# A fused attention and two-layer gated network on one core: most of the gate and value weights prepared later, and the last attention product spread along block 7

## The chip, the core and the metric

The kernel runs on one core of a Trainium2 chip. The core has a matrix engine (TensorE, PE in the profile, with its weight loads as PEld), a vector engine (VectorE, DVE), a scalar engine (ScalarE, ACT), a general engine (GpSimd, POOL) and a queue engine (SyncE, SP). SP and POOL issue the transfers; sixteen DMA engines move the bytes. Each engine takes its instructions in the order in which they stand in its own queue. The metric is the device time of one execution in microseconds (us), the median of three runs.

## The reference, cut to what matters

```python
# attention: 8 batches, 8 heads, 576 tokens, head 64; keys and values are means over 8 tokens
k_p, v_p = mean of 8 tokens of k, v                 # 72 of each
attn = softmax(q @ k_p.T / 8) @ v_p
x = attn as 4608 tokens x 512
# first network
h = ((x @ w1) * (x @ w2)) @ w3                      # 512 -> 1024 -> 1024
y = h @ w_out                                       # 1024 -> 512
# second network
xn = y / sqrt(mean(y*y) + 1e-6) * rms_g
out = (silu(xn @ w_gate) * (xn @ w_val)) @ w_out    # 512 -> 1536 -> 512
```

The weights arrive as 64-bit floats and the result is 32-bit. The kernel computes every large product as three passes of a split operand: high times high, high times low, low times high.

## The kernel before, in words

The 4608 tokens are worked as nine blocks of 512 tokens, numbered 0 to 8, while the attention has eight batches of 576 tokens, numbered 0 to 7. Block i holds the end of batch i-1 and the start of batch i.

**First pass.** `ab(i, m, s)` is one product of block i: twelve matmuls into one PSUM bank, for weight s (0 is w1, 1 is w2) and output part m. A block has sixteen of them. With s = 0 ScalarE copies the bank out (line 571); with s = 1 VectorE multiplies the two (line 574, to tile `hh` or `hl`) and SP stores the result. `w3` and `w_out` were multiplied into one matrix ahead of it (tiles `wph`, `wpl`).

**The attention of the next batch runs between these products.** `positions(i)` is a list of sixteen places, one behind each `ab`. Place 1 holds the last part of the product with the values for block i+1 (`av_step`) and the loads of the keys of the batch after (`C.k0`). Places 1 to 12 hold the scores, the exponentials, the division and the transposes of five token tiles (VectorE's lines 337, 351 to 353 and 368, tile `aT`). Place 13 holds the part of the new batch that lies in block i+1. `av_step` multiplies on TensorE (line 428, bank `pa`), casts on ScalarE (line 435, tile `xh`) and takes the rest on VectorE (line 436, tile `xl`); the block's own matmuls read `xh` (lines 104 and 106) and `xl` (line 105). Places 14 and 15 prepare the keys of the batch after: `C.k1` sums over tokens on VectorE (lines 253 and 257, tile `kv`), `C.kT` turns them on TensorE (line 288), `C.Q` turns the queries (line 307).

**The weights of the second network are prepared in between, too.** `gv_steps(G, s, kp)` makes a group of eight steps for one part of `w_gate` or `w_val`; there are twelve groups (G = 0, 1, 2). Each loads two raw pieces of 0.5 MB (line 127), converts them from 64 to 32 bits (ScalarE's lines 144 and 147, VectorE's 159, 168 and 171), forms four differences (line 733), splits two halves into high and low (lines 100 and 101, tile `wst`) and stores them with four transfers of 0.5 MB from POOL's queue (line 750, to `wd`). A `Ticker` hands out a list of steps evenly over a number of ticks. Before, all 97 steps of the twelve groups are spread over 116 ticks, one behind each `ab` of blocks 1 to 8; what is left is done behind the sixth product of block 8.

**Second pass.** After block 8 the products h are read back (`h_load`, line 1182, tile `hr`), split (`h_split`: ScalarE's line 100, VectorE's line 101, tile `hb`) and multiplied with `wph` and `wpl`. A pair is two parts m, 24 matmuls; the pass has 36 pairs, nine blocks of four. `h_split` is called two pairs ahead, and `hb` has four buffers. `y_end` stores a finished block. In blocks 1 to 5 of this pass a second `Ticker`, `side`, hands out the fourteen steps that convert `w_out` of the second network (twelve conversions, tile `raw`, result `of`, stores to `od`), over 40 ticks.

**Third part.** Block 0 through the second network by `gv`, blocks 1 to 8 by `quad` in pairs of blocks. It reads `wd` (`ring_load`, tile `wr`) and `od` (`o2_load`, tiles `oh`, `ol`).

What a source line calls is not yet the order on an engine: the recording layer sorts the instructions of each engine by its own estimate of when they can start. The orders shown below are those of the built programs.

Of the kernel before, what the change touches and what calls it, by code (L numbers as in the profile page):

```python
# [9 lines left out]
F32 = mybir.dt.float32  # L10
F32R = mybir.dt.float32r
# [10 lines left out]
def kernel(  # L22
# [683 lines left out]
    odram = [dram_p.tile([2, P, 4, DM], F32, name=f"od{g}") for g in range(KF2 // 4)]  # L706
    ready = set()

    def gv_steps(G, s, kp):
        w = (w_gate, w_val)[s]  # L710
        cell = {}

        def ptile(nm, dt=F32R):
            return wC_p.tile([P, 2048], dt, tag="w", name=nm)

        def quart(z):
            if "f" not in cell:
                cell["f"] = ptile("wf", F32).rearrange("p (j f c) -> p j f c", j=2, f=8)
            f = cell["f"].bitcast(I32)
            return f[:, :, 2 + 2 * z : 4 + 2 * z, :]  # L720

        def view(z):
            return z.rearrange("p (j f c) -> p j f c", j=2, f=2)

        def sums():
            f = cell["f"]
            for o, x, y in (
                ("T1", "B12", "B11"),
                ("T2", "B22", "T1"),
                ("T3", "B22", "B12"),  # L730
                ("T4", "B21", "T2"),
            ):
                nc.vector.tensor_tensor(
                    out=f[:, :, FI[o], :],
                    in0=f[:, :, FI[x], :],
                    in1=f[:, :, FI[y], :],
                    op=ALU.subtract,
                )

        def put(j):  # L740
            f = cell["f"]
            c = 2 * G + j
            st = ptile("wst").rearrange("p (f l c) -> p f l c", f=8, l=2)
            split(st[:, :, 0, :], st[:, :, 1, :], f[:, j])
            cell[j] = st

        def store(j):
            c, st = 2 * G + j, cell[j]
            for z in range(2):
                nc.gpsimd.dma_start(  # L750
                    out=wdram[s, c, z][:, :, kp],
                    in_=st[:, 4 * z : 4 * z + 4].bitcast(F32),
                )
            ready.add((s, c, kp))

        cs, raws = [], raw_halves()
        for z in range(2):
            k0 = (2 * z + kp) * P
            src = w[k0 : k0 + P, G * 512 : (G + 1) * 512]
            cs.append(Conv(src, raws, out=lambda z=z: quart(z), view=view))  # L760
            cs[z].on_act = True
        return cs, [
            cs[0].s1,
            cs[0].s2,
            cs[1].s1,
            cs[1].s2,
            sums,
            lambda: put(0),
            lambda: (put(1), store(0)),
            lambda: store(1),  # L770
        ]

    groups = [gv_steps(G, s, kp) for G in range(3) for s in range(2) for kp in range(2)]
    gv_prep = [lambda: [cs_.s0() for cs_ in groups[0][0]]]
    for n, (cs, steps) in enumerate(groups):
        if n + 1 < len(groups):
            nxt = groups[n + 1][0]
            steps[4] = lambda f=steps[4], nxt=nxt: (nxt[0].s0(), nxt[1].s0(), f())
        gv_prep += steps

    def positions(i):
        pos = [[] for _ in range(2 * KF1)]
        b = i + 1
        if b >= B:
            return pos
        A = atts[b]
        pos[1] = av_steps(i, i + 1) + [
            lambda: A.S(0, 0), lambda: A.Q(1, 0), lambda: A.S(0, 1)
        ]
        pos[2] = [lambda: A.N(0)]  # L790
        for t in range(1, NTL):
            p = 2 * t + 1
            pos[p] += [lambda t=t: A.S(t, 0)]
            if t < 4:
                pos[p] += [lambda t=t: A.Q(1 + t // 2, t % 2)]
            pos[p] += [lambda t=t: A.S(t, 1)]
            pos[p + 1] += [
                lambda t=t: A.T(t - 1, 0), lambda t=t: A.T(t - 1, 1), lambda t=t: A.N(t)
            ]
        pos[8] += [A.v]  # L800
        pos[12] += [lambda: A.T(NTL - 1, 0), lambda: A.T(NTL - 1, 1)]
        pos[13] += av_steps(b, i + 1)
        if b + 1 < B:
            C = atts[b + 1]
            pos[1] += [C.k0]
            pos[9] += [C.load_v]
            pos[10] += [lambda: C.q(0)]
            pos[14] += [C.k1, lambda: C.q(1)]
            pos[15] += [C.kT, lambda: C.Q(0, 0), lambda: C.Q(0, 1)]
        return pos  # L810

# [14 lines left out]
            st()  # L826
    xt.pop(0)

    r_p = None
    prep = Ticker(gv_prep, 2 * KF1 * (NB - 2) + 4)  # L830
    for i in range(1, NB):
        if i == NB - 2:
            for st in av_steps(i, i + 1):
                st()
            att.close()
            r_p = ctx.enter_context(tc.tile_pool(name="r", bufs=5, side="right"))
        pos = positions(i)
        for n, (m, s) in enumerate((m, s) for m in range(KF1) for s in range(2)):
            ab(i, m, s)
            for st in pos[n]:  # L840
                st()
            prep()
            if i == NB - 1 and n == 5:
                prep.flush()
                wph[:], wpl[:] = [], []
                for g in range(2):
                    for l, lst in enumerate((wph, wpl)):
                        lst.append(wtile(wC_p, "wp"))
                        nc.sync.dma_start(out=lst[g].bitcast(F32), in_=wpdram[g][l])
        xt.pop(i)  # L850
    h_put.pop(0)()

    def rtile(nm, dt=F32R):
        return r_p.tile([P, 2048], dt, tag="r", name=nm)

    o2r = {}

    def o2_jobs(g):
        cell = {}

        def row(j):
            if j == 0:
                cell["f"] = rtile("of", F32).rearrange("p (j c) -> p j c", j=4)
            return cell["f"].bitcast(I32)[:, j, :]

        def done(_):
            f = cell.pop("f")
            hl = [rtile(nm).rearrange("p (j c) -> p j c", j=4) for nm in ("of", "of")]
            split(hl[0], hl[1], f)
            for l in range(2):  # L870
                nc.gpsimd.dma_start(out=odram[g][l], in_=hl[l].bitcast(F32))

        js = [
            Conv(
                w_o2[(4 * g + j) * P : (4 * g + j + 1) * P, :],
                (r_p, "xq", 2),
                out=lambda j=j: row(j),
                then=done if j == 3 else None,
            )
            for j in range(4)  # L880
        ]
        for j in js:
            j.on_act = True
        return js
# [99 lines left out]
    def xprep(i0):  # L984
        q, rr, sc = {}, {}, {}

        def load():
            rr["r"] = raw_p.tile([P, 1024], I32, tag="raw", name="rr").bitcast(F32)
            for j in range(2):
                nc.sync.dma_start(  # L990
                    out=rr["r"][:, j * TB : (j + 1) * TB],
                    in_=rdram[i0 + j].partition_broadcast(P),
                )
            for j in range(2):
                for u in range(2):
                    if j == 0:
                        t = r_p.tile([P, 1024], I32, tag="xq", name="xq", bufs=2).bitcast(F32)
                    else:
                        t = raw_p.tile([P, 1024], I32, tag="raw", name="xq").bitcast(F32)
                    q[f"A{j + 1}{u + 1}"] = t  # L1000
                    nc.sync.dma_start(
                        out=t.rearrange("p (k t) -> p k t", k=2),
                        in_=ydram[i0 + j, 2 * u : 2 * u + 2].rearrange("k p t -> p k t"),
                    )
# [188 lines left out]
    o2 = []  # L1193
    for g in range(3):
        o2 += o2_jobs(g)
    o2 = conv_steps(o2, 1)
    for n in range(3):
        h_load(n)
    h_split(0)
    h_split(1)  # L1200
    todo = []
    side = Ticker(o2, 5 * KF1)
    xs = xn_steps(0)
    for i in range(NB):
        for m in range(KF1):
            n = i * (KF1 // 2) + m // 2
            if m % 2 == 0:
                h_load(n + 3)
                h_split(n + 2)
            t = hb[n]  # L1210
            h_t[i, m] = [t[:, l, (m % 2) * TB : (m % 2 + 1) * TB] for l in range(2)]
            c = m % 4
            second(i, m, wph[m // 4][:, c, :], wpl[m // 4][:, c, :], KF1 - 1, False)
            if m and todo:
                todo.pop(0)()
            if i == 0 and m == 4:
                ring_load(0, 1)
                ring_load(1, 1)
            if i > 0:
                side()  # L1220
            if i >= NB - 2 and m % 2 and xs:
                xs.pop(0)()
        todo = y_end(i)
# [96 lines left out]
```

## Time and profile before

| | |
|---|---|
| runs | 1677.32, 1675.08, 1678.94 us; median 1677.32 |
| profiled execution | 1674.94 us, of which the span of the trace is 1673.2 us |
| TensorE busy | 1612.5 us of the span |
| VectorE busy | 1012.9 us |
| ScalarE busy | 680.6 us |
| granted clock of TensorE, mean | 0.984 of full speed |
| moved by DMA | 322.52 MB, mean 193 GB/s |

A busy TensorE isn't a TensorE at its peak, since overlapping matmuls count as busy throughout and since its clock is granted at one of two levels. So a stage is read by three columns together: how long TensorE was idle, which clock it was granted, and how busy the engine was that it waited for. Matmuls of 512 columns are listed with 0.39 us each, but they overlap, and start 0.23 us apart.

### The profile page before, as it was taken

The numbers are of one execution on the slowest core, as the hardware profiler recorded it, in microseconds if no ns is written. First come the engines' busy times: TensorE is split into PE (matmuls) and PEld (weight loads), VectorE is DVE, ScalarE is ACT, GpSimd is POOL, SyncE is SP. The second block draws the span as 40 slices with busy tenths as digits, with TensorE's granted clock in tenths as the row PEclk, the third lists the DMA queues.
The fourth block names the chain that finished last, engine by engine and source line by source line (L and its number), as shares of the span: only waits on it lengthen the run. The fifth ranks groups of instructions, "written<-read, shape, count | busy, mean of one in ns | idle before, by whom it ended". The sixth has DMA issues, their size and how long they took to land.

```text
span 1673.2 us, 19957 instructions
## 1 busy us (share of the span) xinstructions
PE 1612.5 (96%) x7250; PEld 1285.4 (77%) x7250; DVE 1012.9 (61%) x1773; ACT 680.6 (41%) x1607; POOL 93.5 (6%) x107
## 2 busy tenths in 40 slices
PE   5899989889889999999999999999999999999999
PEld 2447768678677688888888888888888888888887
DVE  4676698898898632566526253486356735475444
ACT  4776545545445322555423243244323433234321
POOL 1001111211110100000100000000000000000000
PEclk9899999999999899999999999999999999999999
DMA  9858555756853565568556764457345836455422
GB/s 241 253 172 212 136 159 159 194 148 179 207 168 127 175 220 185 189 220 312 187 207 232 277 233 167 164 206 281 151 176 186 297 133 227 160 212 207 176 101 76
DMA packets 147460, 322.52 MB, mean 193 GB/s; under 512 B 52505, under 2 KB 79129, under 8 KB 129442
## 3 DMA queue, kind: packets, MB, share of 16 engines
q1 hardware_dynamic: 126210, 276.13, 48.6%
q0 software_dynamic: 21152, 45.12, 10.1%
q8 instruction: 57, 0.93, 0.2%
q14 instruction: 41, 0.34, 0.1%
HBM read 247.75 MB, written 73.44 MB: 192 GB/s over the span
## 4 chain that ended last, share of the span: by engine, by line
PE 81%; DVE 10%; DMA 4%; issue 2%; ACT 2%; SPq 0%; DVEq 0%; ACTq 0%
PE ps L104 16%; PE ps L105 16%; PE ps L106 16%; PE o L106 5%; PE o L105 5%; PE o L104 5%; DVE aT L368 5%; PE y L106 4%; PE y L104 4%; PE y L105 4%; DMA x1raw<-in_moe_w_out_dram 2%; PE pa L428 2%; PE pa L325 1%; PE wps L626 1%; PE pa L307 1%
## 5 line engine op out<-in xcount | busy, mean ns | idle before, releaser
L104 PE MATMUL ps<-xf,wr 128*128 128x512 f32 x576 | 224.1, 389 | 0.0
L105 PE MATMUL ps<-xf,wr 128*128 128x512 f32 x576 | 224.1, 389 | 0.0
L106 PE MATMUL ps<-xf,wr 128*128 128x512 f32 x576 | 224.1, 389 | 0.0
L104 PE MATMUL o<-oh,hch 128*128 128x512 f32 x384 | 149.4, 389 | 0.0
L105 PE MATMUL o<-ol,hch 128*128 128x512 f32 x384 | 149.4, 389 | 0.0
L106 PE MATMUL o<-oh,hcl 128*128 128x512 f32 x384 | 149.4, 389 | 0.0
L368 DVE STREAM_TRANSPOSE aT<-s 32x256 f32<-32x256 f32 x324 | 140.8, 435 | 4.6
L1078 ACT COPY f<-ps 128x512 f32<-128x512 f32 x144 | 84.5, 586 | 124.7 <-PE ps L106 121.5
L104 PEld LDWEIGHTS ps<-xf,wr 128*128 128x128 f32 x576 | 108.1, 188 | 22.5
L105 PEld LDWEIGHTS ps<-xf,wr 128*128 128x128 f32 x576 | 108.1, 188 | 22.5
L106 PEld LDWEIGHTS ps<-xf,wr 128*128 128x128 f32 x576 | 108.1, 188 | 22.4
L105 PE MATMUL ps<-xl,w1h 128*128 128x512 f32 x288 | 117.1, 407 | 8.1 <-DVE xl L436 8.1
L1082 DVE TENSOR_TENSOR f<-y,f 128x512 f32<-128x512 f32 x48 | 33.2, 692 | 150.1 <-PE y L106 150.1
L104 PE MATMUL ps<-xh,w1h 128*128 128x512 f32 x288 | 119.7, 416 | 0.0
L106 PE MATMUL ps<-xh,w1l 128*128 128x512 f32 x288 | 115.1, 400 | 0.0
L104 PE MATMUL ps<-xh,w2h 128*128 128x512 f32 x288 | 112.8, 392 | 1.4 <-ACT w2h L100 1.4
L106 PE MATMUL ps<-xh,w2l 128*128 128x512 f32 x288 | 112.4, 390 | 0.0
L105 PE MATMUL ps<-xl,w2h 128*128 128x512 f32 x288 | 112.2, 390 | 0.0
L340 ACT ACTIVATE s<-pa,mx 128x72 f32<-128x72 f32 (+1 forms) x280 | 85.8, 333 | 57.9 <-DVE mx L337 57.6
L1102 ACT CAST hch<-f 128x512 fp32r<-128x512 f32 x72 | 44.8, 622 | 105.0 <-DVE f L1096 105.0
L1164 DVE TENSOR_TENSOR acc<-o,acc 128x512 f32<-128x512 f32 x64 | 43.5, 687 | 68.1 <-PE o L106 68.0
L104 PEld LDWEIGHTS o<-oh,hch 128*128 128x128 f32 x384 | 72.1, 188 | 15.0
(194 smaller groups left out, 3255.2 us busy)
## 6 DMA issues: line engine op xcount, KB each, us to landing
wr<-wd SPq DMA_DIRECT2D x96, 1024.0 KB
wd<-wst POOLq DMA_DIRECT2D x48, 512.0 KB, 5.7
hr<-hd SPq DMA_DIRECT2D x36, 512.0 KB
oh<-od SPq DMA_DIRECT2D x15, 1024.0 KB
ol<-od SPq DMA_DIRECT2D x15, 1024.0 KB
wr<-wd SPq DMA_DIRECT2D x24, 512.0 KB
x1raw<-in_moe_w_dram SPq DMA_DIRECT2D x20, 512.0 KB
hd<-hh SPq DMA_DIRECT2D x40, 256.0 KB
```

Source lines behind the costliest of these rows:

```text
L104: nc.tensor.matmul(o, lh, rh, start=first, stop=False, skip_group_check=part)
L105: nc.tensor.matmul(o, lh, rl, start=False, stop=False, skip_group_check=part)
L106: nc.tensor.matmul(o, ll, rh, start=False, stop=last, skip_group_check=part)
L307: nc.tensor.transpose(ps[:, p * P : p * P + n], qt[:n, hf, p * P : (p + 1) * P], ident[:n, :n],)
L325: nc.tensor.matmul(ps[:n, (p % 2) * 2 * SP : (p % 2 + 1) * 2 * SP], qT_t[t // 2][:, t % 2, p, :n], kT[:, p, :], start=True, stop=True,)
L340: nc.scalar.activation(s_t[t][:n, h, :SP], pv[:, j, :], AF.Exp, bias=mx[:, j, :], accum_out=den_t[t][:n, h, :],)
L368: nc.vector.transpose(aT[32 * kb : 32 * kb + 32, :, s0 + 32 * i : s0 + 32 * i + 32], s_t[t][32 * i : 32 * i + 32, :, 32 * kb : 32 * kb + 32],)
L428: nc.tensor.matmul(ps[j * D : (j + 1) * D, :n], st8["vp", b][:, h * D : (h + 1) * D], st8["aT", b][:SP, h, c0 : c0 + n], start=True, stop= ...
L1078: nc.scalar.copy(t, bank)
L1082: nc.vector.tensor_tensor(out=t, in0=bank, in1=t, op=ALU.add)
L1102: nc.scalar.copy(hi, hf)
L1164: nc.vector.tensor_tensor(out=a, in0=ys[j], in1=a, op=ALU.add)
```

## The change

The twelve groups are cut into two lists. The first, the four groups of G = 0 with 33 steps, is spread over 94 ticks in blocks 1 to 6 and flushed there. The second, the eight groups of G = 1 and 2 with 65 steps, is joined with the fourteen steps of `w_out` and spread by `side` over 82 ticks: two at the end of block 7, sixteen in block 8, and 64 in blocks 0 to 7 of the second pass. The later groups take their raw tiles and their results from the pool `r` (five buffers, and two for raw pieces, `xq`) in place of `wC`. `wph` and `wpl` are loaded again in block 7 in place of block 8. `C.k1` moves from place 14 to place 11. The four `av_step` of batch 7 for block 8 stood together ahead of block 7; now one stands behind each second product of block 7.

```diff
     def gv_steps(G, s, kp):
         w = (w_gate, w_val)[s]
         cell = {}
 
+        late = G > 0
+
         def ptile(nm, dt=F32R):
+            if late:
+                return rtile(nm, dt)
             return wC_p.tile([P, 2048], dt, tag="w", name=nm)
...
-        cs, raws = [], raw_halves()
+        cs, raws = [], (xq_raw if late else raw_halves())
...
-    gv_prep = [lambda: [cs_.s0() for cs_ in groups[0][0]]]
+    preps = [[], []]
     for n, (cs, steps) in enumerate(groups):
-        if n + 1 < len(groups):
+        gv_prep = preps[n >= 4]
+        if n in (0, 4):
+            gv_prep.append(lambda cs=cs: [cs_.s0() for cs_ in cs])
+        if n + 1 not in (4, len(groups)):
...
-            pos[14] += [C.k1, lambda: C.q(1)]
+            pos[11] += [C.k1, lambda: C.q(1)]
...
-    prep = Ticker(gv_prep, 2 * KF1 * (NB - 2) + 4)
-    for i in range(1, NB):
-        if i == NB - 2:
-            for st in av_steps(i, i + 1):
-                st()
-            att.close()
-            r_p = ctx.enter_context(tc.tile_pool(name="r", bufs=5, side="right"))
+    prep = Ticker(preps[0], 2 * KF1 * (NB - 3) - 2)
+    for i in range(1, NB - 2):
         pos = positions(i)
...
+    prep.flush()
+    wph[:], wpl[:] = [], []
+    for g in range(2):
+        for l, lst in enumerate((wph, wpl)):
+            lst.append(wtile(wC_p, "wp"))
...
-    o2 = conv_steps(o2, 1)
+    side = Ticker(preps[1] + conv_steps(o2, 1), 18 + KF1 * (NB - 1))
+    for i in range(NB - 2, NB):
+        for n, (m, s) in enumerate((m, s) for m in range(KF1) for s in range(2)):
+            ab(i, m, s)
+            if i == NB - 2 and n < 2 * NP and n % 2:
+                av_step(i, i + 1, n // 2)
+            if i == NB - 2 and n == 2 * NP:
+                att.close()
+                r_ps.append(ctx.enter_context(tc.tile_pool(name="r", bufs=5, side="right")))
+            if i == NB - 2 and n == 10:
+                for g in range(2):
+                    for l, lst in enumerate((wph, wpl)):
+                        nc.sync.dma_start(out=lst[g].bitcast(F32), in_=wpdram[g][l])
+            if (i, n) > (NB - 2, 13):
+                side()
+        xt.pop(i)
+    h_put.pop(0)()
...
-    side = Ticker(o2, 5 * KF1)
...
-            if i > 0:
-                side()
+            side()
```

**VectorE where block 2 ends and block 3 begins, before.** `aT` is the last tile of the attention, `xl` with 320 columns the operand that block 3 waits for, `kv` the sums over the keys of the batch after.

```order
L101 TENSOR_TENSOR wst<-wf,wst 128x8x128
L368 STREAM_TRANSPOSE aT<-s_120 32x8x32 x6
L574 TENSOR_TENSOR hl<-ps,f 128x512
L436 SCALAR_TENSOR_TENSOR xl_2124<-pa,xh_2123 128x320 x4
L253 TENSOR_TENSOR kv<-kv 72x4x128
L168 TENSOR_SCALAR f<-f 128x512
L257 TENSOR_TENSOR kv<-kv 72x2x128
L253 TENSOR_TENSOR kv<-kv 72x4x128
L574 TENSOR_TENSOR hh<-ps,f 128x512
L257 TENSOR_TENSOR kv<-kv 72x2x128
```

The same place in the changed kernel:

```order
L253 TENSOR_TENSOR kv<-kv 72x4x128
L368 STREAM_TRANSPOSE aT<-s_120 32x8x32
L257 TENSOR_TENSOR kv<-kv 72x2x128
L253 TENSOR_TENSOR kv<-kv 72x4x128
L368 STREAM_TRANSPOSE aT<-s_120 32x8x32
L257 TENSOR_TENSOR kv<-kv 72x2x128
L368 STREAM_TRANSPOSE aT<-s_120 32x8x32 x4
L159 SCALAR_TENSOR_TENSOR rawp<-rawp 128x512
L574 TENSOR_TENSOR hl<-ps,f 128x512
L171 ISA wf<-rawp,f 128x2x512
L436 SCALAR_TENSOR_TENSOR xl_2091<-pa,xh_2090 128x320 x4
```

The four sums over keys moved from behind `xl` to among the last transposes, ahead of `xl`.

**VectorE at the end of the second pass, before.** The `hb` rows are the splits of the last four pairs, `xr` and `xnl` the normalised input of the third part, `L664` to `L675` the end of a block.

```order
L101 TENSOR_TENSOR hb<-hr,hb 128x1024
L939 SCALAR_TENSOR_TENSOR xnl_6777<-xr,g_col,xnh_6776 128x512 x2
L935 TENSOR_TENSOR xr<-xr,f 128x512 x2
L939 SCALAR_TENSOR_TENSOR xnl_6777<-xr,g_col,xnh_6776 128x512 x2
L101 TENSOR_TENSOR hb<-hr,hb 128x1024 x2
L664 COPY hl<-ps 128x512
L667 TENSOR_TENSOR f<-f 128x512
L664 COPY hl<-ps 128x512
L667 TENSOR_TENSOR f<-f 128x512 x2
L101 TENSOR_TENSOR hb<-hr,hb 128x1024
```

The changed kernel just ahead of its last pair; `xq` and `f` are the raw and half-converted pieces of `w_out`, `of` the result:

```order
L171 ISA of<-xq,f 128x1024
L159 SCALAR_TENSOR_TENSOR xq<-xq 128x512
L942 SCALAR_TENSOR_TENSOR xnl_6770<-xr,g_col,xnh_6769 128x512
L168 TENSOR_SCALAR f<-f 128x512
L938 TENSOR_TENSOR xr<-xr,f 128x512
L171 ISA of<-xq,f 128x1024
L938 TENSOR_TENSOR xr<-xr,f 128x512
L942 SCALAR_TENSOR_TENSOR xnl_6770<-xr,g_col,xnh_6769 128x512
L938 TENSOR_TENSOR xr<-xr,f 128x512
L159 SCALAR_TENSOR_TENSOR xq<-xq 128x512
L168 TENSOR_SCALAR f<-f 128x512
L101 TENSOR_TENSOR hb<-hr,hb 128x1024
```

The split of the last pair now stands behind `L159` and `L168` of the last of the twelve conversions of `w_out`; the first of the twelve stands behind the split of the 28th pair.

## Rows read from the trace of the kernel before

**Rows 1.** The page: span, and busy time of two engines.
```profile
span 1673.2 us, 19957 instructions
PE 1612.5 (96%) x7250; PEld 1285.4 (77%) x7250; DVE 1012.9 (61%) x1773; ACT 680.6 (41%) x1607; POOL 93.5 (6%) x107
```

**Rows 2.** Busy time in stretches: blocks 1 to 6, then blocks 1, 3, 6 alone.
```profile
core 0: us, PE busy (x) PEld busy (x) DVE busy (x) ACT busy (x) POOL busy (x), PEclk, DMA share, GB/s
187.60:563.80 376.20, 349.27 (x1736) 275.69 (x1733) 331.15 (x739) 181.59 (x681) 54.32 (x60) 0.96 0.60 166
187.60:246.60 59.00, 54.01 (x280) 43.07 (x278) 51.44 (x119) 29.41 (x113) 7.84 (x8) 0.98 0.62 160
309.90:374.80 64.90, 60.54 (x296) 48.51 (x296) 56.94 (x127) 30.53 (x113) 9.48 (x11) 0.96 0.59 158
497.00:563.80 66.80, 63.37 (x303) 46.99 (x303) 58.47 (x128) 31.99 (x116) 5.84 (x8) 0.93 0.42 142
```

**Rows 3.** TensorE's waits from 182 to 570: total, times, longest.
```profile
PE pa L288 <- issue: 15.4, 5, 5.3
PE ps L105 <- DVE xl L436: 8.1, 3, 3.1
PE pa L428 <- DVE xl L436: 3.4, 1, 3.4
```

**Rows 4.** VectorE in order of time at the start of block 4: start, length.
```profile
370.07 1.41 DVE L436 SCALAR_TENSOR_TENSOR xl<-pa,xh 128x256 fp32r<-128x256 f32 x4
...
375.80 0.41 DVE L257 TENSOR_TENSOR kv<-kv 72x256 f32<-72x256 f32 x1
```

**Rows 5.** Stretches of 5 us around the start of block 3.
```profile
305.00:310.00 5.00, 0.08 (x1) 0.11 (x2) 4.94 (x12) 0.00 (x0) 0.40 (x1) 0.88 1.00 337
310.00:315.00 5.00, 5.00 (x19) 4.31 (x20) 2.65 (x5) 1.98 (x4) 0.71 (x1) 0.50 0.59 185
315.00:320.00 5.00, 5.00 (x25) 3.72 (x26) 1.12 (x2) 1.86 (x4) 1.74 (x2) 0.94 0.85 204
```

**Rows 6.** The second pass as one stretch, columns as before.
```profile
651.00:852.80 201.80, 201.80 (x890) 165.16 (x889) 107.83 (x141) 93.33 (x136) 13.31 (x13) 1.00 0.63 217
```

**Rows 7.** VectorE's groups by line, 246 to 498 (blocks 2 to 5).
```profile
L101 DVE TENSOR_TENSOR wst<-wf,wst 128x1024 fp32r<-128x1024 f32 x14 | 16.9, 1216 | 6.1 <-ACT wst L100 6.1
...
L253 DVE TENSOR_TENSOR kv<-kv 72x512 f32<-72x512 f32 x17 | 11.5, 679 | 0.0
...
L733 DVE TENSOR_TENSOR wf<-wf 128x256 f32<-128x256 f32 x28 | 10.8, 416 | 0.2
L159 DVE SCALAR_TENSOR_TENSOR rawp<-rawp 128x512 int32<-128x512 int32 x13 | 8.8, 675 | 0.0
L171 DVE CUSTOM_DVE_ANT_0 wf<-rawp,f 128x1024 uint16<-128x1024 uint16 x13 | 8.6, 665 | 0.2
L168 DVE TENSOR_SCALAR f<-f 128x512 int32<-128x512 int32 x14 | 5.9, 422 | 8.1 <-ACT f L147 8.1
...
L257 DVE TENSOR_TENSOR kv<-kv 72x256 f32<-72x256 f32 x9 | 3.7, 412 | 0.0
```

**Rows 8.** TensorE in order of time, last matmuls of the second pass.
```profile
842.80 0.39 PE L104 MATMUL y<-hb,wp 128*128 128x512 f32 x1
...
845.52 0.39 PE L104 MATMUL y<-hb,wp 128*128 128x512 f32 x1
...
852.60 0.39 PE L106 MATMUL y<-hb,wp 128*128 128x512 f32 x1
```

**Rows 9.** Transfers issued: a group's stores, and those of `w_out`.
```profile
wd<-wst POOLq DMA_DIRECT2D x48, 512.0 KB, 5.7
...
od<-of POOLq DMA_DIRECT2D x6, 1024.0 KB, 9.0
```

**Rows 10.** ScalarE in the second pass: three conversions in a row, the last split.
```profile
756.67 0.67 ACT L144 ACTIVATE raw<-raw 128x512 int32<-128x512 uint32 x1 [3.29 <-DMA raw<-in_moe_w_out_dram]
...
762.83 0.66 ACT L144 ACTIVATE raw<-raw 128x512 int32<-128x512 uint32 x1 [4.00 <-DMA raw<-in_moe_w_out_dram]
...
767.98 0.67 ACT L144 ACTIVATE raw<-raw 128x512 int32<-128x512 uint32 x1 [2.54 <-DMA raw<-in_moe_w_out_dram]
...
831.79 1.09 ACT L100 CAST hb<-hr 128x1024 fp32r<-128x1024 f32 x1
```

**Rows 11.** Two stretches of the second pass with the DMA engines full.
```profile
759.90:765.40 5.50, 5.50 (x26) 4.31 (x25) 1.62 (x4) 2.57 (x4) 0.00 (x0) 1.00 1.00 416
781.70:787.20 5.50, 5.50 (x26) 4.31 (x25) 4.61 (x7) 3.50 (x7) 0.54 (x1) 1.00 1.02 403
```

More of the change, by code (lines that the diff above doesn't have):

```diff
@@ L707, with rtile, xq_raw @@
     ready = set()
+    r_ps = []
+    def rtile(nm, dt=F32R):
+        return r_ps[0].tile([P, 2048], dt, tag="r", name=nm)
+    def xq_raw():
+        return r_ps[0].tile([P, 1024], I32, tag="xq", name="xq", bufs=2)
     def gv_steps(G, s, kp):
@@ L827 @@
     xt.pop(0)
-    r_p = None
-    prep = Ticker(gv_prep, 2 * KF1 * (NB - 2) + 4)
-    for i in range(1, NB):
-        if i == NB - 2:
-            for st in av_steps(i, i + 1):
-                st()
-            att.close()
-            r_p = ctx.enter_context(tc.tile_pool(name="r", bufs=5, side="right"))
+    prep = Ticker(preps[0], 2 * KF1 * (NB - 3) - 2)
+    for i in range(1, NB - 2):
         pos = positions(i)
@@ L842 @@
             prep()
[L843 to L849, printed above, removed]
-        xt.pop(i)
-    h_put.pop(0)()
-    def rtile(nm, dt=F32R):
-        return r_p.tile([P, 2048], dt, tag="r", name=nm)
+        xt.pop(i)
+    prep.flush()
[3 more added lines that the diff above has]
+            lst.append(wtile(wC_p, "wp"))
     o2r = {}
@@ L875, in o2_jobs @@
                 w_o2[(4 * g + j) * P : (4 * g + j + 1) * P, :],
-                (r_p, "xq", 2),
+                xq_raw,
                 out=lambda j=j: row(j),
@@ L996, in load @@
                     if j == 0:
-                        t = r_p.tile([P, 1024], I32, tag="xq", name="xq", bufs=2).bitcast(F32)
+                        t = xq_raw().bitcast(F32)
                     else:
```

## The prediction

> **What bounds the kernel now.** I read the page first: TensorE is busy for 1612.5 of 1673.2 us [rows 1], so 60.7 us of idle time and whatever a lowered clock costs are all that a reordering can win. Then I read busy time by stretches. In blocks 1 to 6 TensorE is busy for 349.27 of 376.20 us, at a mean clock of 0.96, while VectorE is busy for 331.15 us [rows 2]. TensorE's waits in that stretch add up to the same gap: 15.4 + 8.1 + 3.4 = 26.9 us [rows 3]. Two of the three name VectorE's line 436 (`xl`). The largest, on line 288, says "issue", which names nothing; there I went to VectorE's own order of time. At the start of block 4 `xl` ends at 371.48 (370.07 + 1.41) and the last sum over keys, which line 288 turns, at 376.21 [rows 4], with splits of the prepared weights between them. So both waits are VectorE running late at the end of a block. The stretches around block 3 show the same: TensorE busy 0.08 us while VectorE is busy 4.94 of 5 [rows 5].
>
> The stall costs a second time. After the idle stretch 305 to 310 the granted clock is 0.50 for 5 us and 0.94 in the next 5: half speed, the lower of the two levels (1.2 of 2.4 GHz), and 2.8 us of matmul work lost in one boundary (0.50 x 5 + 0.06 x 5) [rows 5]. Over blocks 1 to 6 the clock takes (1 - 0.96) x 376.2 = 15 us. Idle and clock together: 26.9 + 15 = 42 us. That is the most that these blocks can give. Of the 376.2 us, 334 are matmul work.
>
> The second pass has no such loss: busy 201.80 of 201.80 us at full clock, VectorE at 107.83 [rows 6].
>
> **The change part by part.**
>
> *Weights leave blocks 1 to 6.* Over 246 to 498 a group of steps costs VectorE two splits, four differences and two conversions; the five lines sum to 16.9 + 10.8 + 8.8 + 8.6 + 5.9 = 51.0 us for 14 splits, so seven groups, 7.3 us each [rows 7]. Before, 96 of 116 ticks fall in blocks 1 to 6, so 97 x 96 / 116 = 80 steps, ten groups. Now four groups. VectorE loses 6 x 7.3 = 44 us there, 7.3 per block. Its load falls from 331 to 287 us, against 334 us of matmul work; it goes from the engine that sets the block to one with 14% of room.
>
> *The key sums move ahead of `xl`.* Two pairs of 0.68 and 0.41 us, 2.2 us per block (means of lines 253 and 257 [rows 7]). They stop being what line 288 waits for, but they now delay `xl` by those 2.2 us. So `xl` comes 7.3 - 2.2 = 5.1 us earlier per block, and the sums much earlier. The waits on `xl` were 3.1 and 3.4 us at the longest [rows 3], so 5.1 covers them; line 288 held TensorE for 5.3 us at the longest, and there `xl` had ended some us before the sums, as in [rows 4].
>
> *What stays.* VectorE idles 2.35 and 3.88 us in the two stretches behind a stall [rows 5], because a block's first scores aren't there yet. That stays in part, and the four groups don't fall evenly on six blocks. I bound the gain of the blocks by 42 (all) and by 21 (every boundary keeps half its wait and half its low clock), and take 37: a rest of under a us per boundary, which is nearer to the upper end because the load falls by more than any `xl` wait.
>
> *The attention product of batch 7 for block 8.* It stood alone ahead of block 7, behind the 3.4 us wait on line 428 [rows 3]. Its matmuls stay, its four casts and four `xl` now lie beside block 7, where nothing else is left for VectorE but eight products. No cost; its wait is in the 42.
>
> *The eight late groups, first half.* 18 ticks in blocks 7 and 8 and 64 in the second pass, 79 steps in 82 ticks. Steps 1 to 65 are the groups, so six groups fall in the first 49 ticks of the second pass. A tick there is twelve matmuls, 845.52 - 842.80 = 2.72 us [rows 8]. VectorE gets 6 x 7.3 = 44 us more: 152 of 202. It is hidden by the matmuls, with the next split called two pairs (10.9 us) ahead. Transfers: each group loads two raw pieces and stores four of 0.5 MB [rows 9], 3.1 MB, so 19 MB for six on top of the 44 MB that the pass moves now (217 GB/s over 201.8 us) at a share of 0.63 [rows 6]. By the same share that is 0.90. Tight, but under one.
>
> *The fourteen steps of `w_out`.* They now come last: ticks 68 to 82, 15 ticks of 2.72 us, 41 us in place of 109 (40 ticks). This is where I expect the price. Three conversions in a row started at 756.67, 762.83 and 767.98, each behind its raw piece [rows 10], 5.7 us apart with the DMA engines full [rows 11]; ScalarE and VectorE take work in order, so what stands behind a late conversion is late. The built order has the first conversion behind the split of the 28th pair, and the split of the last, 36th, pair behind the twelfth. A split can start when its buffer comes free, four pairs back: the last one started at 831.79 [rows 10], so the 28th starts eight pairs of 5.44 us earlier, at 788.3, and the first conversion at 789.4. The twelfth starts 11 x 5.7 = 62.7 us later, at 852.1, and takes two ScalarE steps of 0.67, VectorE's 0.42 and the split of 1.2 us [rows 7, 10]: the operand is there at 855.1. The last pair begins 24 matmuls before the end, at 847.4 [rows 8]. Late by 7.7 us; with a low clock behind it (2.8 us, as above) 10 us. If conversions follow at 5.0 us, it costs nothing; at 7.0 us it is 22 + 3 = 25. The value taken is that of the rows, 10. What queues behind is the end of blocks 7 and 8 and the last `xnl`, which the third part needs next, so I put no second stall beside it.
>
> Here a page bears on the price. The Trainium skill, "DMA: Bandwidth & Descriptors", Specifications, gives a core about 358 GB/s from its memory. The trace disagrees over short stretches, with 416 and 403 GB/s [rows 11], and the measurement decides. By the page, the some 22 MB that I estimate for those 62 us (twelve raw pieces, four stores, pair loads, block ends, the loads of the third part) would take 61 us in place of 55 at 403 GB/s, the price would be about 16 in place of 10, and the time 1656.
>
> *The sum*, on the profiled execution: 1674.9 - 37 + 10 = 1648. The median of the runs shown stands 2.4 us above that execution: 1650.
>
> **The rivals.**
>
> *The end of the second pass costs nothing.* Transfers of raw pieces start a step ahead and the buffers of `hb` give 15.6 us of slack (847.4 - 831.8). It needs conversions at 5.0 us; the shorter gap in the rows is 5.15. For: the lighter DMA load of earlier blocks leaves no backlog. Against: more is moved at once here than in the rows. 1674.9 - 37, and 2.4: 1640.
>
> *VectorE stays late at the boundaries.* For: it takes 4.94 of 5 us when there is a backlog [rows 5], its attention work comes in a lump up to the end of the block, and 2.2 us more now stand ahead of `xl`. Against: 44 us less load. Half the gain, 21: 1674.9 - 21 + 10 + 2.4 = 1666.
>
> *The wait of line 288 isn't VectorE's, so that the move doesn't do what it says.* For: its releaser is "issue". Then 15.4 us and their part of the clock (15 x 15.4 / 26.9 = 8.6) stay, and about 16 of the other 18 us go: 1674.9 - 16 + 10 + 2.4 = 1671. Against: the sums end just as TensorE goes on [rows 4].
>
> *Slower: the conversions of `w_out` wait for the DMA engines.* One mechanism: the second pass's share of 0.90 leaves no room, raw pieces land late, and twelve in-order conversions hold back the splits of the last pairs. It decides from 8.1 us per conversion (11 x 8.1 - 55 + 2.8 = 37, all of the gain). At 9 us: 44 + 3 = 47 us, 1674.9 - 37 + 47 + 2.4 = 1687. For: stores of a group take 5.7 us to land and those of `w_out` 9.0 [rows 9], in the same engines. Against: the longest gap in the rows, with a share of 1.00, was 6.2 us.
>
> **How the numbers follow.** The forecast 0.55, with a range of its own from 1641 to 1659. No price at the end 0.16. VectorE late 0.18. Line 288 not VectorE's 0.04. Slower 0.07. The first four are below the time before by more than 0.2% (3.4 us), about the least that a measurement of this kernel tells from no change, so faster is 0.91 when 0.02 is taken off for their upper tails; the slower case gives 0.06, and same 0.03. The range 1635 to 1671 reaches from all 42 us without a price (1677.3 - 42) to the case of line 288; it leaves out the slower case and the ends.
>
> **What would show it.** Right: TensorE's wait on line 288 gone and its waits on line 436 under 1 us each between blocks; no stretch of clock 0.50 from 240 to 520; blocks 1 to 6 in about 339 us in place of 376; VectorE near 287 us there. In the second pass a wait on `hb` near its last pair of 5 to 10 us, and ScalarE waiting for raw pieces of `w_out` close together, at a DMA share near 1. Wrong: waits on `xl` as long as before at a lower load of VectorE (then the order, not the load, makes it late); TensorE idle in the first 49 ticks of the second pass (then the groups don't hide); or a gap longer than 20 us at its end.

## The result, and the profile after

The changed kernel takes 1660.57 us (median of four runs, 1659.05 to 1663.74), the kernel before in the same job 1676.2 us (also of four): ratio 0.9909, 95% interval 0.9887 to 0.9931. The change is faster by some 15.6 us. The forecast was 1650 in a range from 1635 to 1671: the sign and the range held, the gain came out 11 us smaller.

The page of the kernel after, first lines (answers to [rows 1]):

```profile
span 1662.0 us, 19939 instructions
...
PE 1609.1 (97%) x7250; PEld 1281.7 (77%) x7250; DVE 1018.0 (61%) x1773; ACT 680.1 (41%) x1607; POOL 93.1 (6%) x107
```

The profiled execution took 1663.74 us, the slowest of the four. It was late before the change begins: block 0's first product starts at 130.46 us against 127.06, and in other profiled kernels with the same code up to there at 122 to 130. So I compare stretches and not ends. Each block begins with VectorE's first product (line 574), and the last stretch runs from block 8's last product to the last matmul of the third part on `xnh` and `wr`; behind that all these profiles agree within 1 us, before and after within 0.1. Two numbers then carry the change, and they explain the median: -33.2 + 17.0 = -16.2.

| us | before | after |
|---|---|---|
| blocks 1 to 6 | 379.3 | 341.9 |
| block 7 | 43.6 | 48.4 |
| blocks 1 to 8 together | 461.6 | 428.4 |
| from there to the last `xnh` matmul | 291.2 | 308.2 |

Blocks 1 to 6, then block 1, block 3 and block 6 alone, of the kernel after (columns as in [rows 2]):

```profile
197.30:539.20 341.90, 335.92 (x1718) 269.77 (x1716) 291.91 (x663) 152.71 (x638) 35.01 (x35) 1.00 0.52 138
197.30:254.50 57.20, 56.17 (x291) 44.87 (x288) 51.38 (x116) 27.09 (x109) 5.31 (x6) 1.00 0.45 111
310.20:367.50 57.30, 55.92 (x290) 45.05 (x288) 48.53 (x113) 26.05 (x107) 7.89 (x9) 1.00 0.55 136
485.80:539.20 53.40, 53.40 (x272) 43.09 (x270) 42.61 (x100) 20.65 (x99) 1.87 (x3) 1.00 0.42 154
```

VectorE works 39 us less and TensorE's clock is back at 1.00. What TensorE still waits for there, total, times and longest, against the three lines of [rows 3]:

```profile
PE pa L288 <- DVE xl L436: 6.0, 4, 2.6
```

26.9 us of waits became 6.0. The lines 105 and 428 are gone, and line 288, which said "issue" in [rows 3], now names `xl`: it seems that the transposes of the keys want a bank that the attention product before them still holds (`kT_early`, below, takes them out from behind it, and these waits go). The worst boundary left, in stretches of 5 us (the 0.50 of [rows 5] is a 0.66 here):

```profile
415.00:420.00 5.00, 2.38 (x16) 1.78 (x15) 4.90 (x14) 3.47 (x7) 0.00 (x0) 1.00 0.06 23
420.00:425.00 5.00, 5.00 (x19) 4.15 (x18) 2.76 (x3) 1.61 (x5) 2.98 (x5) 0.66 0.77 222
```

The second pass, in which TensorE never stopped before [rows 6], now has stops. The whole pass, then stretches of 3 us in it:

```profile
626.00:835.50 209.50, 201.75 (x879) 164.05 (x878) 146.35 (x209) 114.11 (x164) 31.00 (x37) 0.98 0.84 283
799.00:802.00 3.00, 0.92 (x5) 0.42 (x3) 3.00 (x6) 0.71 (x1) 0.00 (x0) 1.00 1.02 406
802.00:805.00 3.00, 0.51 (x1) 0.08 (x1) 1.37 (x3) 2.28 (x4) 0.00 (x0) 0.56 1.03 393
805.00:808.00 3.00, 2.86 (x8) 2.21 (x8) 2.50 (x4) 0.38 (x1) 0.00 (x0) 0.50 0.88 269
820.00:823.00 3.00, 1.07 (x5) 0.56 (x3) 1.41 (x3) 0.63 (x2) 0.00 (x0) 1.00 0.89 313
```

TensorE's waits from 625 to 870 of the kernel after:

```profile
PE y L681 <- ACT f L673: 4.6, 1, 4.6
PE y L104 <- ACT f L684: 3.0, 1, 3.0
PE y L104 <- ACT hh L100: 1.8, 1, 1.8
PE ps L104 <- DMA wr<-wd: 1.6, 1, 1.6
```

The names need a second look. The order of time of all engines around the first two stops shows what the named instruction itself stood behind (start, length, engine, line, tiles, idle time before it and its releaser):

```profile
802.72 0.65 ACT L144 ACTIVATE xq<-xq 128x512 int32<-128x512 uint32 x1 [3.01 <-DMA xq<-in_moe_w_out_dram]
803.28 0.64 ACT L147 ACTIVATE f<-xq 128x512 f32<-128x512 f32 x1
803.83 0.61 ACT L673 CAST f<-f 128x512 fp32r<-128x512 f32 x1
...
804.49 0.59 PE L681 MATMUL y<-f,ones 128*1 128x512 f32 x1 [4.57 <-ACT f L673]
...
822.37 0.67 ACT L144 ACTIVATE xq<-xq 128x512 int32<-128x512 uint32 x1 [2.66 <-DMA xq<-in_moe_w_out_dram]
...
823.07 0.69 DVE L159 SCALAR_TENSOR_TENSOR xq<-xq 128x512 int32<-128x512 int32 x1 [1.66 <-ACT xq L144]
823.50 0.56 ACT L684 COPY f<-y 1x512 f32<-1x512 f32 x1
823.68 0.42 DVE L168 TENSOR_SCALAR f<-f 128x512 int32<-128x512 int32 x1
...
824.01 1.22 DVE L101 TENSOR_TENSOR hb<-hr,hb 128x1024 fp32r<-128x1024 f32 x1
...
824.11 0.50 PE L104 MATMUL y<-hb,wp 128*128 128x512 f32 x1 [3.04 <-ACT f L684]
```

In both, ScalarE sat idle for a raw piece of `w_out`, with the step that TensorE needs queued behind the conversion: the cast of line 673, then the copy of line 684. That copy empties one of the four banks `y`, in which the sums of squares of a block lie, and the block after the next needs all four; the product goes on 0.05 us after the copy ends (824.06). The last pair's split of `hb` stood behind the same conversion's two steps on VectorE, but it held nothing: it ended at 825.23, no wait of TensorE names `hb`, and the last 24 matmuls of the pass, as many as a pair has, began at 829.68.

### The profile page after: what moved, and what is told of

It reads as the page before. It is cut to its first block, busy times and chain, and to the rows that moved or that the text cites. A ratio compares the mean times of both kernels' runs of the same rounds, so it can differ in the third digit from the quotient of the medians.

```text
span 1662.0 us, 19939 instructions
## 1 busy us (share of the span) xinstructions
PE 1609.1 (97%) x7250; PEld 1281.7 (77%) x7250; DVE 1018.0 (61%) x1773; ACT 680.1 (41%) x1607; POOL 93.1 (6%) x107
## 5 line engine op out<-in xcount | busy, mean ns | idle before, releaser
L1085 DVE TENSOR_TENSOR f<-y,f 128x512 f32<-128x512 f32 x48 | 33.2, 691 | 149.9 <-PE y L106 149.9
L1167 DVE TENSOR_TENSOR acc<-o,acc 128x512 f32<-128x512 f32 x64 | 43.5, 687 | 68.1 <-PE o L106 68.1
L626 PE MATMUL wps<-wo,hl 128*128 128x512 f32 x128 | 68.9, 664 | 16.6 <-ACT hl L559 9.6
```

Source lines behind the costliest of these rows:

```text
L626: nc.tensor.matmul(wps[i], wt[:, i * P : (i + 1) * P], wo[j // 4][:, j % 4, :], start=j == 0, stop=j == KF1 - 1,)
L1085: nc.vector.tensor_tensor(out=t, in0=bank, in1=t, op=ALU.add)
L1167: nc.vector.tensor_tensor(out=a, in0=ys[j], in1=a, op=ALU.add)
```

## The experiments

Each is an edit of the kernel after, except the first. Two columns show where the time lies, as in the table above.

| run | time, us | ratio to before | interval | blocks 1 to 8 | to last `xnh` |
|---|---|---|---|---|---|
| before | 1676.2 | | | 461.6 | 291.2 |
| after | 1660.57 | 0.9909 | 0.9887 to 0.9931 | 428.4 | 308.2 |
| k1_alone | 1676.4 | 1.0007 | 0.9989 to 1.0026 | 462.1 | 291.2 |
| late_alone | 1676.02 | 1.0007 | 0.9991 to 1.0024 | 441.1 | 311.0 |
| av_together | 1658.56 | 0.9915 | 0.9893 to 0.9938 | 427.2 | 309.8 |
| wout_first | 1660.16 | 0.9918 | 0.9896 to 0.994 | 444.3 | 296.1 |
| wout_wide | 1650.66 | 0.9866 | 0.9844 to 0.9889 | 428.6 | 299.0 |
| kT_early | 1658.4 | 0.9905 | 0.9879 to 0.993 | 427.1 | 309.7 |
| combined | 1648.53 | 0.9842 | 0.9821 to 0.9864 | 426.7 | 299.3 |
| wout_done48 | 1650.72 | 0.9836 | 0.9822 to 0.9851 | 428.3 | 297.3 |
| combined2 | 1647.15 | 0.9819 | 0.9803 to 0.9836 | 426.2 | 298.8 |
| eight_early | 1667.44 | 0.9937 | 0.9923 to 0.9951 | 452.2 | 291.9 |
| combined3 | 1641.82 | 0.9806 | 0.9784 to 0.9828 | 426.0 | 292.5 |
| key_chain_back | 1641.18 | 0.9793 | 0.9765 to 0.9821 | 427.1 | 291.8 |

**The key sums by themselves** (the kernel before with the one move):

```diff
-            pos[14] += [C.k1, lambda: C.q(1)]
+            pos[11] += [C.k1, lambda: C.q(1)]
```

> The kernel before with the key sums at place 11 in place of 14, and nothing else. Theory (VectorE's load makes the waits at the block ends): the load is unchanged, the wait of line 288 turns into a wait on xl, time 1671 to 1676 us. Rival (the place of the sums makes them): the 15.4 us of line 288 and their clock go, 1664 us or less.

The theory held: nothing. TensorE's waits in the blocks, from 185 to 570:

```profile
PE pa L288 <- DVE xl L436: 24.0, 5, 5.6
PE pa L428 <- DVE xl L436: 3.4, 1, 3.4
```

The sums are no longer the last, and line 288 now waits for `xl` instead: 27.4 us in all, 26.9 in [rows 3]. While VectorE is behind, it doesn't matter which of its results is asked for last.

**The rest by itself** (after, with the sums back at place 14):

```diff
-            pos[11] += [C.k1, lambda: C.q(1)]
+            pos[14] += [C.k1, lambda: C.q(1)]
```

> The changed kernel with the key sums back at place 14. Theory (load): the gain of blocks 1 to 6 stays but for 1 or 2 us per boundary, 1661 to 1668 us. Rival (place): the waits of line 288 come back as in the kernel before, and with the price at the end of the second pass the time is 1672 to 1680 us.

The theory's total fell and the rival's came, but by two stages that nearly cancel: -20.5 in the blocks and +19.8 behind them. TensorE's waits in the blocks, from 185 to 545:

```profile
PE pa L288 <- issue: 8.4, 3, 3.7
PE pa L288 <- DVE kv L257: 4.4, 5, 1.6
```

With the load gone, the order counts: line 288 waits 12.8 us, 4.4 of them put down to the sums and 8.4 to nothing named, where the kernel after has 6.0, and blocks 1 to 6 take 354.5 against 341.9. So the move that is worth nothing alone is worth 12.6 us in these blocks behind the other.

**The attention product of the eighth batch in one piece**, its four steps together ahead of block 7:

```diff
+    for st in av_steps(NB - 2, NB - 1):
+        st()
+    att.close()
+    r_ps.append(ctx.enter_context(tc.tile_pool(name="r", ...)))
     for i in range(NB - 2, NB):
...
-            if i == NB - 2 and n < 2 * NP and n % 2:
-                av_step(i, i + 1, n // 2)
```

> The changed kernel with the four attention products of batch 7 for block 8 together again, ahead of block 7. Theory: the wait of 3.4 us ahead of them came from VectorE's backlog, which is smaller now, so 2 to 6 us more than the changed kernel, 1662 to 1667 us. Rival (that place alone cost the 8 us of idle time and low clock that stood there): 1668 to 1670 us.

It fell: spreading is worth nothing. Block 6 takes 57.2 and block 7 43.5, together 1.1 less than spread (53.4 and 48.4).

**The `w_out` steps ahead of the late groups.**

```diff
-    side = Ticker(preps[1] + conv_steps(o2, 1), 18 + KF1 * (NB - 1))
+    side = Ticker(conv_steps(o2, 1) + preps[1], 18 + KF1 * (NB - 1))
```

> The changed kernel with the fourteen steps of w_out ahead of the 65 steps of the late groups in the second list, so that they run in blocks 7 and 8. Theory (the price at the end of the second pass is that of splits and casts queued behind the conversions of w_out): 11 us of idle time and 5 us of low clock there go to under 5, 1643 to 1650 us. Rival (the second pass moves too much whatever the order): the stalls stay or move, 1656 to 1663 us.

The end of the second pass lost 4.9 us in place of 17.0, but the time stayed, so the rival came. In stretches of 3 us, inside block 8 now:

```profile
602.00:605.00 3.00, 0.64 (x3) 0.19 (x1) 0.00 (x0) 0.00 (x0) 0.00 (x0) 1.00 1.00 381
605.00:608.00 3.00, 0.41 (x1) 0.41 (x2) 1.46 (x3) 2.17 (x5) 0.00 (x0) 0.50 1.04 414
```

Hardly an engine computes from 602 to 605 while the transfers run at 381 to 414 GB/s. ScalarE in order of time tells why:

```profile
605.83 0.65 ACT L144 ACTIVATE xq<-xq 128x512 int32<-128x512 uint32 x1 [10.35 <-DMA xq<-in_moe_w_out_dram]
606.38 0.68 ACT L147 ACTIVATE f<-xq 128x512 f32<-128x512 f32 x1
606.95 0.59 ACT L571 COPY f<-ps 128x512 f32<-128x512 f32 x1
```

The copy out of the bank (line 571) stands behind a conversion that waited 10.35 us for its raw piece. The stop goes where the conversions go, as long as they come a step per row.

**Two paces.** Late groups first, over 47 ticks; `w_out` steps 2.6 rows apart behind them.

```diff
-    side = Ticker(preps[1] + conv_steps(o2, 1), 18 + KF1 * (NB - 1))
+    lateg = Ticker(preps[1], 47)
+    side = Ticker(conv_steps(o2, 1), 36)
...
-            if (i, n) > (NB - 2, 13):
-                side()
+            if (i, n) > (NB - 2, 8):
+                lateg()
...
-            side()
+            if i * KF1 + m < 24:
+                lateg()
+            else:
+                side()
```

> The changed kernel with two separate paces: the eight late groups spread over 47 ticks (from the ninth row on of block 7 to the 24th row of the second pass, 1.4 steps a tick), and only then the fourteen w_out steps, 36 ticks for 14 steps, one every 2.6 rows (about 7 us apart, where the changed kernel has 2.7). Theory: the stalls follow the w_out steps because at one step per 2.7 us row each conversion waits for a raw piece that was asked for only one step before, and the copy or split behind it then comes late; with 7 us between steps the pieces are there, so most of the 17 us that the changed kernel loses at the end of the second pass and the start of the third part come back: 1648 to 1654 us, TensorE waits for L673, L684 and L104 splits gone there. Rival: the loss is set by the amount of traffic and of conversion work laid into blocks 7, 8 and the second pass, wherever it lies; then the denser late groups stall TensorE instead, and the time stays at 1657 to 1664 us.

The theory held in total, ten us less than after. What remains is one stop, from 799 to 811. TensorE waits 4.4 us for line 684 again and goes on 0.05 us behind it; this time the copy stood on ScalarE behind line 941, which had waited 10.30 us for the residual rows (line 938):

```profile
799.00:811.00 12.00, 7.56 (x24) 5.75 (x23) 11.16 (x17) 8.49 (x14) 0.29 (x1) 0.72 0.55 208
```

**The key chain further up**, ahead of the attention product.

```diff
-            pos[10] += [lambda: C.q(0)]
-            pos[11] += [C.k1, lambda: C.q(1)]
-            pos[15] += [C.kT, lambda: C.Q(0, 0), lambda: C.Q(0, 1)]
+            pos[8] += [lambda: C.q(0)]
+            pos[9] += [C.k1, lambda: C.q(1)]
+            pos[12] += [C.kT, lambda: C.Q(0, 0), lambda: C.Q(0, 1)]
```

> The changed kernel with the next batch's key chain moved up by more places: q loads at place 8, k sums and second q load at 9, the transposes kT and Q at place 12, before the AV products at 13 (instead of 10, 11 and 15, behind them). Theory: the 6.0 us that TensorE still waits in blocks 1 to 6 for xl at L436 are waits for a bank that the AV products hold while VectorE is late; ahead of the AV products the transposes need no such bank, so those waits and about 2 us of lowered clock go: 1651 to 1656 us. Rival: VectorE is late there whatever the order, and the AV products or the sums get the wait instead (L428 or L288 for kv): 1658 to 1663 us.

The rival came: waits on `xl` gone, others in their place, 2 us or nothing. From 192 to 545:

```profile
PE pa L288 <- DVE kv L257: 3.1, 3, 1.2
PE pa L288 <- PE ps L106: 1.4, 2, 0.7
```

**The three together** (`wout_wide`, `kT_early`, `av_together`):

> Both of the above and the eighth batch's AV products together ahead of block 7. Theory: the two gains are in different stages and add, 12 to 20 us less than the changed kernel: 1640 to 1649 us. Rival: one of them is taken back elsewhere (waits shift to the stage of the other, or the late groups stall TensorE): 1651 to 1660 us.

At the upper end of the theory's range. The table shows whose gain it is: 9 us of it lie behind the blocks, and the two edits of the blocks bring 1.7 in the blocks.

**Both paces earlier**: 39 and 32 ticks, `w_out` done with the 48th of 72 rows.

```diff
-    lateg = Ticker(preps[1], 47)
-    side = Ticker(conv_steps(o2, 1), 36)
+    lateg = Ticker(preps[1], 39)
+    side = Ticker(conv_steps(o2, 1), 32)
...
-            if i * KF1 + m < 24:
+            if i * KF1 + m < 16:
```

> The two separate paces of wout_wide, both shifted forward: the late groups over 39 ticks (1.7 steps a row, done with the 16th row of the second pass), the fourteen w_out steps over the 32 rows behind (one every 2.3 rows, 6.2 us), so that the last store of w_out pieces is issued near the 48th row, before the residual rows of the third part are asked for at the 50th. In wout_wide TensorE still stood 4.4 us near 802 us and ran at half clock behind it: the multiply of the residual rows xr waited for its transfer, which shared full queues with the last two w_out stores, and the last hidden-row split stood behind it. Theory: with those stores over, that stop and its clock go, 6 to 8 us less than wout_wide: 1642 to 1646 us. Rival: at 1.7 steps a row the late groups themselves make TensorE wait (the transfer share was already 1.0 in stretches of 640 to 700 us), or the xr transfer is late whatever lies beside it: 1649 to 1656 us.

The residual rows are asked for behind the 58th row; the "50th" of the expectation is a slip. The stop at 800 is gone, but the rival came: at 1.7 steps a row TensorE stops where the late groups end, 664 to 676, with the transfers full. The wait is for line 684 once more, behind the first conversion of `w_out`.

```profile
664.00:676.00 12.00, 8.63 (x31) 6.66 (x31) 9.40 (x15) 8.68 (x14) 2.94 (x4) 0.86 1.02 393
...
670.26 0.66 ACT L144 ACTIVATE xq<-xq 128x512 int32<-128x512 uint32 x1 [1.12 <-DMA xq<-in_moe_w_out_dram]
670.83 0.56 ACT L684 COPY f<-y 1x512 f32<-1x512 f32 x1
...
671.44 0.76 PE L104 MATMUL y<-hb,wp 128*128 128x512 f32 x1 [3.37 <-ACT f L684]
```

**That, with the two small edits**:

> wout_done48 with the two edits that showed 0 to 2 us each: the key chain moved up (kT_early) and the eighth batch's AV products together ahead of block 7. Theory: 1 to 3 us less than wout_done48: 1640 to 1645 us. Rival: nothing more, the two are within noise: equal to wout_done48 within 1 us.

1647.15, short of the theory's 1640 to 1645 and 3.6 us under `wout_done48`. In the traces the blocks gain 2.1 us and the stretch behind them loses 1.5, so the rival, nothing more, isn't excluded.

**Eight groups early, four late** (on `wout_done48`):

```diff
-        late = G > 0
+        late = G > 1
...
-        gv_prep = preps[n >= 4]
+        gv_prep = preps[n >= 8]
```

> wout_done48 with eight groups instead of four prepared in blocks 1 to 6, and four late ones over the same 39 ticks. It tells whether the loss in blocks 1 to 6 grows with VectorE's load or sets in from a point. Theory: the waits are a queue's on VectorE, and grow faster than its load: 29 us more VectorE work in six blocks (331 of 376 us before with twelve groups, some 287 with four) gives back about a third to a half of the 37 us gained there: 12 to 19 us over wout_done48, blocks 1 to 6 at 354 to 361 us. Rival: in proportion, 18.7 us for half of the eight groups, is the upper end of that; a threshold near twelve groups would show 0 to 5 us, blocks 1 to 6 at 342 to 347 us, and then fewer late groups cost nothing.

16.7 us over `wout_done48`, as the theory had it, but the blocks alone give more than its 354 to 361. Blocks 1 to 6 take 365.6 us:

```profile
196.90:562.50 365.60, 343.56 (x1718) 275.91 (x1718) 316.50 (x709) 169.05 (x661) 47.45 (x51) 0.97 0.58 161
```

No threshold: eight groups' work in these blocks takes 365.6, four 341.9. Ten (the kernel before) take 379.3, of which 3.8 us are the eighth batch's attention product (57.2 - 53.4, `av_together`), which the other two have in block 7: 375.5 like for like. That is 9.9 / 2 = 5.0 and 23.7 / 4 = 5.9 us for each group, most of VectorE's own 7.3; in proportion to the groups the eight would give 341.9 + 33.6 x 4 / 6 = 364.3. With four late groups the stretch behind the blocks is back at 291.9. Here their pace is halved with their number (33 steps over the same 39 ticks), and this run can't tell the two apart; the next two come to 292.5 and 291.8 with all eight late, so the number need not cost anything.

**A slower pace for the late groups, done as early**: they begin with block 7's second row, over 47 ticks (on `combined2`).

```diff
-    lateg = Ticker(preps[1], 39)
+    lateg = Ticker(preps[1], 47)
...
-            if (i, n) > (NB - 2, 8):
+            if (i, n) > (NB - 2, 0):
```

> combined2 with the late groups begun at the second row of block 7 (the AV products stand together ahead of it, so the buffers are free) and spread over 47 ticks, 1.4 steps a row as in wout_wide, but done with the 16th row of the second pass and the w_out steps done with the 48th as in wout_done48. At 1.7 steps a row (wout_done48) TensorE lost 3.4 us and some clock between 660 and 680 us, with the transfer share at 1.0 there; at 1.4 but w_out ending late (wout_wide) it lost 4.4 us near 802 us. Theory: each stop has its own cause, a pace too dense for the transfers and a last store beside the residual rows, so with both avoided neither comes: 5 to 8 us less than combined2, 1639 to 1643 us, no wait of TensorE over 1 us in the second pass. Rival: the work laid into blocks 7, 8 and the second pass costs its stop wherever there is least room, so another takes its place: 1645 to 1650 us.

The theory held: 1641.82, and no wait of TensorE over 0.3 us in the second pass.

**The key chain back** where the kernel after has it, the rest as in `combined3`:

> combined3 with the key chain at the places of the changed kernel again (second query load, sums at 11, transposes kT and Q at 15 behind the AV products); pacing and the joined AV products stay. In combined3 the AV products of block 0 waited 7.1 us behind the copies of kT and qT on ScalarE (2.7 in the changed kernel), while blocks 1 to 6 gained 1 us. Theory: the key chain moved up is worth nothing or a little less, since its transposes take the banks that the AV products wait for: 1638 to 1642 us. Rival: it is worth what kT_early showed against the changed kernel, some 2 us, and block 0 varies by execution: 1643 to 1646 us.

1641.18, the same as `combined3`: the further move of the key chain is worth nothing. Blocks 1 to 6, the end of the first pass, and the second pass with the start of the third part:

```profile
195.10:540.70 345.60, 339.74 (x1734) 271.24 (x1733) 294.82 (x667) 156.43 (x644) 35.05 (x35) 1.00 0.52 140
560.00:660.00 100.00, 100.00 (x443) 82.82 (x442) 69.53 (x108) 47.76 (x69) 17.43 (x24) 1.00 0.88 299
660.00:870.00 210.00, 210.00 (x926) 171.71 (x925) 114.40 (x158) 92.28 (x139) 17.49 (x18) 1.00 0.71 247
```

This is the version that beats both: 0.9793 of before, 19 us under the kernel after, with the same work in the same stages. Only the places differ.

## Why the prediction was right, and where its size was not

- **Blocks 1 to 6, -37.** The stretch is 379.3 - 341.9 = 37.4 us shorter, but 3.8 us of that (57.2 - 53.4) is the eighth batch's attention product, which now lies in block 7. Like for like the first pass gained 33.2 us, 4 less than forecast. The prediction had the `xl` waits covered, under 1 us each; four are left, 6.0 us in all and 2.6 at the longest. That the load makes the waits is shown by `late_alone` and `eight_early`. The groups took ScalarE's casts and transfers with them, too; that it is VectorE's part of the load rests on [rows 5], where VectorE works 4.94 of 5 us and ScalarE none while TensorE stands, and on the 39 us less on VectorE (44 forecast).
- **The sums moved ahead.** Right that line 288 no longer waits for them; the 6.0 us it still waits for `xl` were not foreseen. `k1_alone` shows that they are worth nothing until the load is gone.
- **The attention product beside block 7, no cost.** Right to a us: 1.1 (`av_together`).
- **The late groups hidden in the first 49 ticks.** Right: TensorE is busy 20.00 of 20 us in each slice from 620 to 780 of the kernel after.
- **The twelve conversions at 5.7 us.** They start from 760.63 to 822.37: 61.74 / 11 = 5.6 us apart on the mean, with gaps from 1.1 to 13.6. The stops behind them add up to 4.6 + 3.0 = 7.6 us, where 7.7 was worked out, and the second pass lost 11.0 us, with the low clock, where 10 was. The size held, the path did not: the price was worked out for the last pair, waiting for its split (`hb`), and no wait on `hb` came. TensorE stood for lines 673 and 684, two steps of a block's end, behind the eighth and the twelfth conversion. Without these stops it would have come to the last pair 11.0 us earlier, at 818.7, and the split of 825.23 would have held it 6.5 us (an estimate from these times, with the conversions where they were). So the cause, conversions that hold back an engine working in order, is the forecast one; that 7.6 meets 7.7 is partly luck.
- **"I put no second stall beside it": this step failed.** The third part's first matmuls lost another 6.0 us, 1.8 for a split and 1.6 for its weights `wr`, the rest at a lowered clock. The first of the two on VectorE, in order of time:

```profile
844.53 0.69 DVE L675 TENSOR_TENSOR f<-f 128x512 fp32r<-128x512 f32 x1 [1.89 <-DMA sdram<-f]
846.98 0.17 DVE L688 TENSOR_SCALAR ss<-ss 128x4 f32<-128x4 f32 x1 [1.76 <-DMA ss<-sdram]
847.08 0.69 DVE L981 TENSOR_TENSOR f<-ps,f 128x512 f32<-128x512 f32 x1
```

  A product (line 981) and the split behind it stand behind two steps that wait for transfers of 2 KB, with the DMA engines at a share of 1.00 from 843 to 846. The prediction had named the end of the blocks, then left it at nothing. In `wout_wide`, where the last stores lie earlier, this stretch costs nothing, and the third part up to its last `xnh` matmul takes 92.3 us, as before, against 98.3.

The sum: 4 us of the blocks, 6 at the third part and 1 in the second pass make the 11 us between forecast and result. The 1656 that the prediction works out beside its own time lies nearer, but not by its reason: the conversions came 5.6 us apart, as forecast, and the transfers of the stop ran at 406 and 393 GB/s. The rivals are settled as well: "the end costs nothing" and "VectorE stays late" fell by the rows above, and line 288's wait was VectorE's. The slower case, conversions at 9 us, did not come. But without the moved sums the load moved late gives back nearly all that it gains (`late_alone`, 19.8 of 20.5 us).

What stays open: whether in the kernel after the late raw pieces come from the bytes in flight or from their being asked for only one step ahead. A longer lead was not tried. Nor was a copy of line 684 ahead of the conversions, or a bank of its own for these sums, though a stop in each of three kernels hangs on that copy (the kernel after, `wout_wide`, `wout_done48`).

## What to carry to other kernels

Work that is moved off a bound engine is paid for again where it lands if a conversion there waits for its input: on an engine that works in order, everything behind it is late. So lay such work out by the pace at which its transfers can land, end it before the next stage asks for its first data, and give the steps that load a pace of their own. Test a move both alone and with the others: here one edit was worth 0 alone and 12.6 us behind the other.

## What the runs showed of the hardware

- Transfers ran at 406 and 393 GB/s (the kernel after) and 381 and 414 GB/s (`wout_first`) in 3-us stretches of a stop, and a 2 KB row written to memory and read back held VectorE for 1.89 and 1.76 us beside a DMA share of 1.00.
- The clock's answer to a stop varies. In and behind the stop of 4.6 us the granted clock was 0.56 and 0.50 for two stretches of 3 us; behind that of 3.0 us it stayed at 1.00, and behind that of 1.8 us it fell to 0.69. Here are the stretches behind the last two, of the kernel after:

```profile
826.00:829.00 3.00, 3.00 (x15) 2.46 (x14) 2.87 (x5) 3.00 (x5) 0.32 (x1) 1.00 0.81 265
...
849.00:852.00 3.00, 3.00 (x9) 2.23 (x9) 1.44 (x3) 0.62 (x1) 0.00 (x0) 0.69 0.95 271
```

- Removed load on VectorE came back for the greater part as time, 5.0 to 5.9 us of 7.3 per group, although VectorE was busy for only 88% of blocks 1 to 6 (331.15 of 376.20, [rows 2]): it bounds the block ends, where its work comes in a lump.
